# One load, two pieces and GpSimd's scaling for the forget gates of an attention and feed-forward kernel

## The chip, the cores and the metric

The kernel runs on one core of a Trainium2 chip. A core has five engines that run side by side, each with its own queue of instructions: TensorE (PE in the profile, PEld for its weight loads), VectorE (DVE), ScalarE (ACT), GpSimd (POOL) and SyncE (SP), which here only issues transfers (DMAs). They wait for each other by semaphores. The metric is the time of one execution on the device in microseconds (us); lower is better.

## The reference

For 8 batches and 8 heads the reference computes causal attention with a learned decay, and feeds the result through a low-rank token mix and a two-layer perceptron:

```
scores = q @ k^T / 8                                  (576 x 576 per head)
cum    = cumsum(log(clip(f, 1e-4, 1)))                (f: 8 x 8 x 576 forget gates)
attn   = softmax(causal(scores + cum[:, None] - cum[None, :]))
x      = attn @ v                                     (heads side by side: 8 x 576 x 512)
u      = x + (x^T @ U @ V)^T                          (rank 32)
out    = u + relu(u @ w_ch1) @ w_ch2                  (512 -> 2048 -> 512)
```

The softmax runs over the columns of a row, so cum of the row drops out; what is added to the scores is minus cum of the column. Only this matters here: `f` is small (64 rows of 576 numbers), and its clipped, logged and summed form `cum` is needed before the first softmax can be taken.

## The kernel before, in words

Two heads make a pair; there are 32 pairs, and a pair's two heads lie on partitions 0 to 63 and 64 to 127. The attention of the pairs, and the first 6 of 16 column blocks of the perceptron, run in the first some 740 us; the rest of the perceptron follows. The change touches only the beginning.

The beginning (lines 903 to 945) is written by hand, in this order:

- TensorE: 12 products of a constant (line 904), then products of the identity that only keep it running (`keep_awake`, line 868), then the first scores of pair 0. For the pairs 0 and 1 a block of scores is two products for each head: q with k (line 538), and a selector with the sums of the gates (line 544), which adds -8 times `cum` of the pair's head in the same PSUM bank. The selector is the tile `picks`, the sums are the tile `fr`.
- SyncE: loads the gates `f` into `fr` twice, once onto each half of the partitions (line 906); then k, q and the last rows of q of pair 0, the first block of w1, and so on.
- VectorE clips `fr` (line 931), ScalarE takes its logarithm into `fl` (line 932), VectorE sums along the row with a scan back into `fr` (line 934), then writes -8 times the first 64 rows into `fl` (line 935). SyncE stores that to the DRAM tensor `cumd` (line 945), from which the pairs from 2 on load their decay: `decay`, for line 500.
- GpSimd meanwhile fills the masks of pairs 0 and 1 with `affine_select`: four triangles (line 513, in widths of 1024, 512, 256 and 768 columns) and two corners (line 517), then clears rows of `xn` (line 937).

From there on the order of the instructions comes from a planner in the kernel (`run`). Each piece of work is an `op` with a planned duration on one or more engines, a priority and keys that it reads and writes; the planner keeps a clock for each engine and takes the op with the best priority among those that could start. Keys that the hand-written beginning makes, such as `("fr",)` and `("fl",)`, are declared with `known` and a planned time. The engines then run each its own list in that order, and wait where the data is not there yet.

The first softmax work of pair 0 is VectorE's line 556 (add the mask, take the extreme of a row), then ScalarE's line 562 (exponential). Beside it the weights are unpacked: line 385 on ScalarE, 397, 398, 402 and 403 on VectorE, 413 and 417 on GpSimd.

Of the kernel before, what the change touches and what calls it, by code (L numbers as in the profile page):

```python
# [22 lines left out]
P = 128  # L23
# [13 lines left out]
NF = 6  # L37
# [14 lines left out]
def tile_decay_attention_moe(ctx, tc, qk, v, f, U, V, w1, w2, out):  # L52
# [154 lines left out]
    FB_ = [psF.tile([P, 512], F32, tag="F", name=f"F{x}") for x in range(2)]  # L207
    busy = FB_[0]
    still = ident.bitcast(BF16)
    NP = B * NHP  # L210
    cur = [UH, UL]

# [19 lines left out]
    def op(alts, pr, r=(), w=(), opens=(), uses=(), mode=None, lands=None, behind=(), ease=0.0):  # L232
        o = Op()
        o.alts, o.pr, o.opens, o.uses, o.mode, o.lands = alts, pr, opens, uses, mode, lands
        o.gives, o.ready, o.n, o.end, o.group = [], 0.0, state["n"], None, state["group"]
        state["n"] += 1
        need = set()
        for k in r:
            if k in writer:
                need.add(writer[k])  # L240
        for k in w:
            if k in writer:
                need.add(writer[k])
            need.update(readers.get(k, ()))
        for k in r:
            readers.setdefault(k, []).append(o)
        for k in w:
            writer[k], readers[k] = o, []
        need.discard(o)
        o.needs, o.ease = 0, ease  # L250
        for k in behind:
            x = writer.get(k)
            if x is not None and x.end is None and x not in need:
                o.needs += 1
                x.gives.append((o, False))
        for x in need:
            if x.end is None:
                o.needs += 1
                x.gives.append((o, True))
            else:  # L260
                o.ready = max(o.ready, x.end)
        for bank in (*opens, *uses):
            bank.left += 1
        todo.append(o)
        return o
# [10 lines left out]
    def load(pr, nbytes, fn, r=(), w=()):  # L276
        return op([("SP", 0.45, fn)], pr, r, w, lands=nbytes / 200e3)
# [205 lines left out]
    def inputs(p):  # L483
        raw, R = RAW[p % 2], ("raw", p % 2)
        if p:
            pr = p - 1.5
            load(pr, 295e3, lambda: nc.sync.dma_start(raw[:, KO:QW], qk[p, :, 1]), w=[(R, "k")])
            load(pr, 262e3, lambda: nc.sync.dma_start(raw[:, 0:MAIN], qk[p, :, 0, 0:MAIN]), w=[(R, "q")])
            for j in range(2):
                load(pr, 16e3, lambda j=j: nc.sync.dma_start(raw[OWN[j], QT + 64 * j : QT + 64 * j + 64], qk[p, OWN[j], 0, MAIN:S]), w=[(R, "t", j)])  # L490
        if p >= NF:
            h, l = Q
            for n, c, k in ((S, slice(KO, QW), ["k"]), (KO, slice(0, KO), ["q", "t"])):
                kr = [(R, "k")] if k == ["k"] else [(R, "q"), (R, "t", 0), (R, "t", 1)]
                op([("ACT", 0.06 + 0.00088 * n, lambda c=c: nc.scalar.copy(h[:, c], raw[:, c]))], p - 0.5, kr, [("qh", k[0]), ("fr",)])  # L495
                op([("POOL", 0.1 + 0.00225 * n, lambda c=c: nc.gpsimd.tensor_tensor(l[:, c], raw[:, c], h.bitcast(F32)[:, c], op=ALU.subtract))],  # L496
                   p - 0.5, kr + [("qh", k[0])], [("ql", k[0]), *(("picks", x) for x in range(NPK))])
        if p >= NPK:
            src = cumd.rearrange("(j p) s -> p j s", j=2)[p, :, 0:MAIN]
            load(p - 1.0, 524e3, lambda: nc.sync.dma_start(decay, src.unsqueeze(0).broadcast_to([P, 2, MAIN])), r=[("cumd",)], w=[("decay",)])  # L500
            for j in range(2):
                load(p - 0.9, 147e3, lambda j=j: nc.sync.dma_start(Mt[OWN[j]], cumd[j * NP + p].unsqueeze(0).broadcast_to([64, S])), r=[("cumd",)], w=[("Mt", j)])
            for i, d in ((3, 1.0), (1, 0.57), (0, 0.37), (2, 0.79)):
                op([("POOL", d, lambda i=i: triangle(i))], p - 0.4, [("decay",)], [("M", i)])
            for j in range(2):
                op([("POOL", 0.24, lambda j=j: corner(j))], p - 0.3, (), [("Mt", j)])
        vr = VR[p % 2]
        load(p - 0.6, 262e3, lambda: nc.sync.dma_start(vr[:, 0:NM], v[p, 0:MAIN].rearrange("(c p) d -> p c d", p=P)), w=[("vr", p % 2, 0)])
        load(p - 0.6, 33e3, lambda: nc.sync.dma_start(vr[64:128, NM], v[p, MAIN:S]), w=[("vr", p % 2, 1)])
# [15 lines left out]
    def scores(p, parts, pr):  # L525
        ts, bank = terms(p), [Bank("S") for _ in range(2 * len(parts))]
        items = [(i, off, bank[2 * x : 2 * x + 2]) for x, part in enumerate(parts) for i, off in part]
        nm, sm = NMX[p % 2], SMX[p % 2]
        R = ("raw", p % 2)
        kr = [(R, "k"), (R, "q")] if p < NF else [("qh", "k"), ("qh", "q"), ("ql", "k"), ("ql", "q")]  # L530
        cost = sum(P * (i + 1) * (0.00168 if p < NF else 0.00136) + 0.02 for i, _, _ in items) * (2 if p < NPK else 1)

        def go():
            for i, off, own in items:
                w = P * (i + 1)
                for m, (q, k) in enumerate(ts):
                    for j in range(2):
                        nc.tensor.matmul(  # L538
                            own[j][:, off : off + w], q[OWN[j], P * i : P * i + P], k[OWN[j], KO : KO + w],
                            start=m == 0, stop=p >= NPK and m == len(ts) - 1,  # L540
                        )
                if p < NPK:
                    for j in range(2):
                        nc.tensor.matmul(
                            own[j][:, off : off + w], picks[OWN[j], p, 0:P], fr[OWN[j], 0:w], start=False, stop=True
                        )

        op([("PE", cost, go)], pr, kr + ([("fr",), ("picks", p)] if p < NPK else []), [(own[j], i) for i, _, own in items for j in range(2)], opens=bank, mode="S")
        for i, off, own in items:
            w = P * (i + 1)  # L550
            for j in range(2):
                col = 2 * i + j

                def top(own=own, i=i, j=j, off=off, w=w, col=col):
                    ps = own[j][:, off : off + w]
                    nc.vector.tensor_tensor_reduce(  # L556
                        ps, ps, Ms[i][:, j], scale=-SCALE, scalar=3.0e38,
                        op0=ALU.add, op1=ALU.min, accum_out=nm[:, col : col + 1],
                    )

                def use(own=own, i=i, j=j, off=off, w=w, col=col):
                    nc.scalar.activation(  # L562
                        PP[i][j], own[j][:, off : off + w], AF.Exp, bias=nm[:, col : col + 1], scale=-1.0, accum_out=sm[:, col : col + 1]
                    )

                op([("DVE", 0.075 + 0.00105 * w, top)], pr + 0.02, [("M", i)], [(own[j], i), ("nm", p % 2, col)], uses=[own[j]])
                op([("ACT", 0.23 + 0.00088 * w, use)], pr + 0.03, [(own[j], i), ("nm", p % 2, col)], [("P", i, j), ("sm", p % 2, col)], uses=[own[j]])

    def score_tail(p, pr):
# [13 lines left out]
                if p < NPK:  # L583
                    nc.tensor.matmul(ps, picks[:, p, P : 2 * P], fr[:, HW * x : HW * x + HW], start=False, stop=True)

        op([("PE", 0.96 * (2 if p < NPK else 1) if p < NF else 0.8, go)], pr, kr + ([("fr",), ("picks", p)] if p < NPK else []), [(bank[x], 4) for x in range(2)], opens=bank, mode="F")
        for x in range(2):

            def top(x=x):
# [312 lines left out]
    with tc.manual_schedule(engines=None):  # L902
        for _ in range(12):
            nc.tensor.matmul(busy, warm[:, 0:P], warm, start=True, stop=True)
        for j in range(2):
            nc.sync.dma_start(fr[OWN[j]], f)
        raw = RAW[0]
        nc.sync.dma_start(raw[:, KO:QW], qk[0, :, 1])
        nc.sync.dma_start(raw[:, 0:MAIN], qk[0, :, 0, 0:MAIN])
# [18 lines left out]

        for x in range(4):
            pick(0, x)  # L930
        nc.vector.tensor_scalar(fr, fr, 1e-4, 1.0, op0=ALU.max, op1=ALU.min)
        nc.scalar.activation(fl, fr, AF.Ln)
        nc.scalar.activation(fl0, warm[:, P : P + 1], AF.Exp)
        nc.vector.tensor_tensor_scan(fr, fl, fl, 0.0, op0=ALU.add, op1=ALU.bypass)
        nc.vector.tensor_scalar(fl[0 : B * H], fr[0 : B * H], -8.0, None, op0=ALU.mult)
        for i in range(NX - 1):
            nc.gpsimd.memset(xn[i][64:128, NM, :], 0.0)
        known(7.2, ("fr",), ("picks", 0))
        known(7.7, ("fl",), ("warm",))
        known(6.3, (("raw", 0), "k"), (("raw", 0), "q"), (("raw", 0), "t", 0), (("raw", 0), "t", 1))  # L940
        known(5.6, *(("M", i) for i in range(NM)), ("Mt", 0), ("Mt", 1))
        clock.update(PE=6.3, DVE=7.5, ACT=5.4, POOL=6.6, SP=2.7)
        state["pipe"] = 6.0

        load(0.0, 147e3, lambda: nc.sync.dma_start(cumd, fl[0 : B * H]), r=[("fl",)] + [("xl", h) for h in range(2)], w=[("cumd",)])
        for p in range(1, NPK):
            op([("ACT", 1.0, lambda p=p: [pick(p, x) for x in range(4)])], p - 0.6, [("warm",)], [("picks", p)])
# [653 lines left out]
```

## Time and profile before

| what | value |
|---|---|
| median of 3 runs | 1169.71 us (1167.19 to 1170.69) |
| profiled execution: time, and its span | 1169.24 us, 1167.3 us |
| busy over the span: PE, DVE, ACT, POOL | 1144.9, 838.9, 656.8, 312.6 us |
| granted clock of TensorE, mean over the span | 0.998 of full speed |

The span goes from the first to the last instruction that the profile records; the execution's own time has 1.94 us more around it. A busy PE is one that has a product in its pipeline, so that 98% busy does not say that it runs at its peak. In a timeline each row is an instruction, or some equal ones that follow each other: start, duration, engine, line, operation, output and inputs, shapes, and how many. In square brackets stands how long the engine sat idle before the row, and what ended that. PEld is TensorE's loading of weights, which lies beside products that still run; an idle PEld is not an idle PE.

### The profile page before, as it was taken

What the parts mean: (1) busy time and instruction counts of PE and PEld (TensorE: products, weight loads), DVE (VectorE), ACT (ScalarE), POOL (GpSimd) and SP (SyncE); (2) the same over time, 40 slices, a digit from 0 to 9 for tenths busy, and PEclk for the clock granted to TensorE, in tenths of its full rate; (3) what the DMA queues carried; (4) which work ended last, traced back from release to release, by engine and by line L of the source; (5) the groups of instructions that cost most, each with busy time, mean ns of one, the idle gap of its engine ahead of it and who ended that gap; (6) DMA issues with size and microseconds to landing.
All of it is one profiled execution on the core that took longest, in us unless ns stands there. A gap on an engine that the chain in (4) does not pass through costs nothing. (4 is left out here: it accounts for less than half of the span.)

```text
span 1167.3 us, 23653 instructions
## 1 busy us (share of the span) xinstructions
PE 1144.9 (98%) x8380; PEld 999.9 (86%) x8380; DVE 838.9 (72%) x2052; ACT 656.8 (56%) x1760; POOL 312.6 (27%) x439
## 2 busy tenths in 40 slices
PE   9989999999999999999999999999999999999997
PEld 6658778888888888878788898788999999999997
DVE  7999886796786787776877423277777768687765
ACT  7877665666665656665475211246555565655653
POOL 5676554344543436434243000000000000000000
PEclk9999999999999999999999999999999999999999
DMA  6757546555665655566361659347747475564643
GB/s 216 187 156 225 151 145 204 154 182 179 188 196 151 182 189 163 151 208 190 123 201 57 224 191 306 117 160 233 245 158 232 153 248 170 190 214 145 196 117 109
DMA packets 133446, 210.30 MB, mean 180 GB/s; under 512 B 16656, under 2 KB 58896, under 8 KB 131280
## 3 DMA queue, kind: packets, MB, share of 16 engines
q1 hardware_dynamic: 133056, 208.53, 57.2%
q8 instruction: 66, 1.08, 0.4%
q14 instruction: 52, 0.43, 0.1%
q10 hardware_dynamic: 272, 0.26, 0.1%
HBM read 153.03 MB, written 55.72 MB: 179 GB/s over the span
## 5 line engine op out<-in xcount | busy, mean ns | idle before, releaser
L562 ACT ACTIVATE P<-S,nm 128x512 f32<-128x512 f32 (+3 forms) x256 | 132.8, 528 | 62.7 <-DVE nm L556 62.1
L1392 POOL TENSOR_TENSOR xn<-xn,xn 128x512 f32<-128x512 f32 x1 | 1.3, 1267 | 518.7 <-DMA out_dram<-xn 518.7
L556 DVE CUSTOM_DVE_ANT_0 S<-S,M 128x512 f32<-128x512 f32 (+3 forms) x256 | 119.3, 515 | 27.1 <-PE S L538 23.1
L513 POOL TENSOR_SCALAR_AFFINE_SELECT M<-decay 128x1024 f32<-128x1024 f32 (+1 forms) x124 | 93.6, 776 | 108.8 <-DVE nm L556 71.7
L807 PE MATMUL F<-uh,w1h 128*128 128x256 f32 (+1 forms) x344 | 107.4, 312 | 1.1 <-DVE hl L811 1.1
L807 PE MATMUL F<-ul,w1h 128*128 128x256 f32 (+1 forms) x344 | 101.2, 294 | 0.0
L807 PE MATMUL F<-uh,w1l 128*128 128x256 f32 (+1 forms) x344 | 101.1, 294 | 0.0
L274 ACT COPY PT<-T 128x256 f32<-128x256 f32 (+4 forms) x203 | 79.9, 425 | 37.3 <-PE T L629 19.0
L496 POOL TENSOR_TENSOR qkl<-raw,qkh 128x576 fp32r<-128x576 f32 (+1 forms) x52 | 79.5, 1530 | 78.2 <-ACT qkh L495 50.6
L666 PE MATMUL T<-PT,vr 128*64 128x320 f32 (+3 forms) x628 | 90.6, 434 | 2.6 <-DVE PT L274 2.6
L629 PE MATMUL T<-ident,P 128*128 128x128 f32 x614 | 88.0, 275 | 3.3 <-DVE xn L688 2.4
L1464 ACT COPY ost<-pf 128x512 f32<-128x512 f32 x70 | 41.1, 587 | 87.4 <-PE pf L1241 87.4
L1464 ACT COPY mc<-pf 128x512 f32<-128x512 f32 x69 | 40.5, 587 | 81.5 <-PE pf L1241 79.6
L629 PEld LDWEIGHTS T<-ident,P 128*128 128x128 f32 x614 | 69.9, 140 | 18.2 <-DVE xn L688 3.4
L828 PE MATMUL F<-w2h,hh 128*128 128x512 f32 x198 | 84.7, 428 | 0.4 <-DVE ul L754 0.4
L666 PEld LDWEIGHTS T<-PT,vr 128*64 128x64 f32 x628 | 40.7, 138 | 47.6 <-issue 34.1
L828 PE MATMUL F<-w2l,hh 128*128 128x512 f32 x198 | 77.9, 393 | 0.0
L828 PE MATMUL F<-w2h,hl 128*128 128x512 f32 x198 | 77.3, 390 | 0.0
L274 DVE COPY PT<-T 128x512 f32<-128x512 f32 (+4 forms) x103 | 51.4, 506 | 33.9 <-PE T L629 12.0
L1241 PE MATMUL pf<-d,b1h 128*128 128x256 f32 x320 | 69.5, 280 | 0.0
L807 PEld LDWEIGHTS F<-uh,w1h 128*128 128x128 f32 x344 | 65.3, 190 | 4.0 <-DVE hl L811 1.5
L816 ACT ACTIVATE hh<-F 128x256 fp32r<-128x256 f32 (+1 forms) x86 | 34.6, 411 | 56.4 <-PE F L807 56.1
(354 smaller groups left out, 3588.4 us busy)
## 6 DMA issues: line engine op xcount, KB each, us to landing
un<-ud SPq DMA_DIRECT2D x16, 1024.0 KB, 6.5
decay<-cumd SPq DMA_DIRECT2D x30, 512.0 KB, 6.3
d<-ud SPq DMA_DIRECT2D x48, 256.0 KB, 3.8
araw<-in_w_dram SPq DMA_DIRECT2D x20, 512.0 KB, 4.8
wd<-araw SPq DMA_DIRECT2D x20, 512.0 KB, 3.0
raw<-in_qk_dram SPq DMA_DIRECT2D x32, 288.0 KB, 4.2
Th<-twd SPq DMA_DIRECT2D x35, 256.0 KB, 3.6
tw<-twd SPq DMA_DIRECT2D x35, 256.0 KB, 3.0
```

The costliest lines, as they stand in the source:

```text
L274: return [("ACT", 0.133 + 0.00068 * n, lambda: nc.scalar.copy(dst(), src())), ("DVE", 0.064 + 0.00104 * n, lambda: nc.vector.tensor_copy(d ...
L496: op([("POOL", 0.1 + 0.00225 * n, lambda c=c: nc.gpsimd.tensor_tensor(l[:, c], raw[:, c], h.bitcast(F32)[:, c], op=ALU.subtract))], p - 0. ...
L513: nc.gpsimd.affine_select(Ms[i], decay[:, :, 0:w], [[0, 2], [-1, w]], ALU.is_ge, MASKED, base=P * i, channel_multiplier=1)
L556: nc.vector.tensor_tensor_reduce(ps, ps, Ms[i][:, j], scale=-SCALE, scalar=3.0e38, op0=ALU.add, op1=ALU.min, accum_out=nm[:, col : col + 1],)
L562: nc.scalar.activation(PP[i][j], own[j][:, off : off + w], AF.Exp, bias=nm[:, col : col + 1], scale=-1.0, accum_out=sm[:, col : col + 1])
L629: nc.tensor.transpose(bank[:, P * x : P * x + P], PP[i][j][:, P * c : P * c + P], ident)
L666: nc.tensor.matmul(ps, vr[:, c, j], PT[:, j, c, lo:hi], start=c == 0, stop=lo == 0)
L807: nc.tensor.matmul(bank[:, :nt], wt[:, fc, c], ut[:, c, sl], start=m == 0, stop=m == 3 * NDC - 1)
L816: op([("ACT", 0.133 + 0.00066 * nt, lambda: nc.scalar.activation(HH[:, fc, :nt], bank[:, :nt], AF.Relu))], pr, [(bank, 0)], [("hh", fc)], ...
L828: nc.tensor.matmul(bank[:, :], ht[:, fc, P * y : P * y + P], wt[:, fc], start=fc == 0 and m == 0, stop=fc == NA - 1 and m == 2,)
L1241: nc.tensor.matmul(ps, a[x][:, c], b[y][:, c], start=start and m == 0, stop=m == 5, skip_group_check=True)
L1464: nc.scalar.copy(mc, FA)
```

## The change

The gates are loaded by one DMA that reads `f` twice. Clip and logarithm, and after them the sum, go in two pieces of columns, 0 to 255 and 256 to 575; the second sum starts from the last column of the first. The key `("fr",)` becomes one key for each piece; a block of scores asks for the pieces that its columns need. The scaling by -8 leaves VectorE's hand-written beginning, and becomes an op of the planner on GpSimd, planned at 0.8 us, on which the store of `cumd` waits.

```
@@ -207,6 +207,7 @@
+    PIECES = ((0, 2 * P), (2 * P, S))
@@ -545,7 +546,8 @@  (scores)
-        op([("PE", cost, go)], pr, kr + ([("fr",), ("picks", p)] if p < NPK else []), [(own[j], i) for i, _, own in items for j in range(2)], opens=bank, mode="S")
+        upto = [("fr", x) for x, (c0, c1) in enumerate(PIECES) if any(P * (i + 1) > c0 for i, _, _ in items)]
+        op([("PE", cost, go)], pr, kr + ([*upto, ("picks", p)] if p < NPK else []), [(own[j], i) for i, _, own in items for j in range(2)], opens=bank, mode="S")
...
@@ -902,8 +904,7 @@
-        for j in range(2):
-            nc.sync.dma_start(fr[OWN[j]], f)
+        nc.sync.dma_start(fr, f.unsqueeze(0).broadcast_to([2, B * H, S]))
...
@@ -928,20 +929,24 @@
-        nc.vector.tensor_scalar(fr, fr, 1e-4, 1.0, op0=ALU.max, op1=ALU.min)
-        nc.scalar.activation(fl, fr, AF.Ln)
+        for x, (c0, c1) in enumerate(PIECES):
+            c = slice(c0, c1)
+            nc.vector.tensor_scalar(fr[:, c], fr[:, c], 1e-4, 1.0, op0=ALU.max, op1=ALU.min)
+            nc.scalar.activation(fl[:, c], fr[:, c], AF.Ln)
         nc.scalar.activation(fl0, warm[:, P : P + 1], AF.Exp)
-        nc.vector.tensor_tensor_scan(fr, fl, fl, 0.0, op0=ALU.add, op1=ALU.bypass)
-        nc.vector.tensor_scalar(fl[0 : B * H], fr[0 : B * H], -8.0, None, op0=ALU.mult)
+        for x, (c0, c1) in enumerate(PIECES):
+            c = slice(c0, c1)
+            nc.vector.tensor_tensor_scan(fr[:, c], fl[:, c], fl[:, c], fr[:, c0 - 1 : c0] if c0 else 0.0, op0=ALU.add, op1=ALU.bypass)
...
-        known(7.2, ("fr",), ("picks", 0))
+        known(7.2, ("fr", 0), ("fr", 1), ("picks", 0))
...
+        op([("POOL", 0.8, lambda: nc.gpsimd.tensor_scalar(fl[0 : B * H], fr[0 : B * H], -8.0, None, op0=ALU.mult))], 0.2, [("fr", 0), ("fr", 1)], [("fl",)] + [("xl", h) for h in range(2)])
         load(0.0, 147e3, lambda: nc.sync.dma_start(cumd, fl[0 : B * H]), r=[("fl",)] + [("xl", h) for h in range(2)], w=[("cumd",)])
```

VectorE's list at the beginning, from the last constant to the first softmax work of pair 0, stands so in the kernel before (S is a bank of scores, nm the extremes of its rows, M a mask):

```order
L125 MEMSET warm 128x128
L931 TENSOR_SCALAR fr<-fr 128x576
L934 SCALAR_TENSOR_TENSOR fr<-fl 128x576
L935 TENSOR_SCALAR fl<-fr 64x576
L556 ISA S_142,nm_129<-S_142,M_113 128x512
L556 ISA nm_129 128x1
```

and so in the changed one, where lines of the file have moved by one to five (558 is 556 of before):

```order
L125 MEMSET warm 128x128
L934 TENSOR_SCALAR fr<-fr 128x256
L934 TENSOR_SCALAR fr<-fr 128x320
L939 SCALAR_TENSOR_TENSOR fr<-fl 128x256
L939 SCALAR_TENSOR_TENSOR fr<-fl,fr 128x320
L558 ISA S_142,nm_129<-S_142,M_113 128x512
L558 ISA nm_129 128x1
```

Clip and scan are two instructions each, and the scaling is gone from here. GpSimd's list from its last triangle to the first weights, before (`stg` holds raw weights, w1l is the low part of an unpacked block of w1):

```order
L513 AFFINE_SELECT M_112<-decay 128x768
L517 AFFINE_SELECT Mt<-Mt 64x64 x2
L937 MEMSET xn_97 64x512
L937 MEMSET xn_98 64x512
L413 TENSOR_TENSOR stg_202<-stg_202 128x512
L417 TENSOR_TENSOR w1l<-stg_202,w1h 128x512
```

and after the change (414 is 413 of before):

```order
L514 AFFINE_SELECT M_112<-decay 128x768
L518 AFFINE_SELECT Mt<-Mt 64x64 x2
L941 MEMSET xn_97 64x512
L941 MEMSET xn_98 64x512
L949 TENSOR_SCALAR fl<-fr 64x576
L414 TENSOR_TENSOR stg_203<-stg_203 128x512
L418 TENSOR_TENSOR w1l<-stg_203,w1h 128x512
```

The scaling stands behind the two clears, ahead of the first weights. ScalarE has two logarithms in place of one, and SyncE one load in place of two. Every other instruction of all five lists, to the end of the kernel, stands in the same order in both programs.

## Rows read from the trace of the kernel before

**Rows 1.** The page's first part: busy time, share of the span, instructions.

```profile
PE 1144.9 (98%) x8380; PEld 999.9 (86%) x8380; DVE 838.9 (72%) x2052; ACT 656.8 (56%) x1760; POOL 312.6 (27%) x439
```

**Rows 2.** Busy time by stretch: window, length, then PE, PEld, DVE, ACT, POOL.

```profile
16.75:30.00 13.25, 13.25 (x93) 8.70 (x92) 12.87 (x41) 9.67 (x32) 6.97 (x11) 1.00 0.66 220
```

**Rows 3.** Timeline of TensorE, first scores of pair 0.

```profile
5.88 0.82 PE L868 MATMUL F<-ident 128*128 128x256 bf16 x6
6.62 1.13 PE L538 MATMUL S<-raw 64*128 64x512 f32 x4
...
7.49 0.37 PEld L544 LDWEIGHTS S<-fr,picks 64*128 64x128 f32 x4 [0.57 <-DVE fr L934]
7.59 1.10 PE L544 MATMUL S<-fr,picks 64*128 64x512 f32 x4
```

**Rows 4.** Timeline of TensorE, the same work of pair 1.

```profile
16.75 1.13 PE L538 MATMUL S<-raw 64*128 64x512 f32 x4
17.71 1.02 PE L544 MATMUL S<-fr,picks 64*128 64x512 f32 x4
```

**Rows 5.** Timeline of VectorE from the gates' clip to the first weights.

```profile
4.64 0.54 DVE L931 TENSOR_SCALAR fr<-fr 128x576 f32<-128x576 f32 x1 [2.82 <-DMA fr<-in_f_dram]
5.93 1.50 DVE L934 TENSOR_TENSOR_SCAN fr<-fl 128x576 f32<-128x576 f32 x1 [0.75 <-ACT fl L932]
7.47 0.45 DVE L935 TENSOR_SCALAR fl<-fr 64x576 f32<-64x576 f32 x1
8.77 0.70 DVE L556 CUSTOM_DVE_ANT_0 S<-S,M 128x512 f32<-128x512 f32 x1 [0.84 <-PE S L544]
...
10.03 0.43 DVE L397 TENSOR_SCALAR stg<-stg 128x512 int32<-128x512 int32 x1
```

**Rows 6.** Timeline of ScalarE up to the logarithm.

```profile
3.29 1.42 ACT L927 ACTIVATE picks<-warm,ident 64x128 f32<-64x128 bf16 x4 [1.06 <-POOL ident masks.py:199]
5.21 0.69 ACT L932 ACTIVATE fl<-fr 128x576 f32<-128x576 f32 x1 [0.50 <-DVE fr L931]
```

**Rows 7.** Timeline of GpSimd: triangles, a corner, a clear; last a later corner.

```profile
4.22 0.61 POOL L513 TENSOR_SCALAR_AFFINE_SELECT M<-decay 128x512 f32<-128x512 f32 x1
4.79 0.65 POOL L513 TENSOR_SCALAR_AFFINE_SELECT M<-decay 128x256 f32<-128x256 f32 x1
5.40 0.83 POOL L513 TENSOR_SCALAR_AFFINE_SELECT M<-decay 128x768 f32<-128x768 f32 x1
6.19 1.28 POOL L517 TENSOR_SCALAR_AFFINE_SELECT Mt<-Mt 64x64 f32<-64x64 f32 x1
...
8.44 0.52 POOL L937 MEMSET xn<- 64x512 f32 x1
...
33.02 0.23 POOL L517 TENSOR_SCALAR_AFFINE_SELECT Mt<-Mt 64x64 f32<-64x64 f32 x1
```

**Rows 8.** Timeline of SyncE's issues.

```profile
0.74 1.22 SPq L906 DMA_DIRECT2D fr<-in_f_dram  x2
...
8.95 0.47 SPq L945 DMA_DIRECT2D cumd<-fl  x1
...
12.68 0.52 SPq L490 DMA_DIRECT2D raw<-in_qk_dram  x1
14.96 0.35 SPq L487 DMA_DIRECT2D raw<-in_qk_dram  x1
...
17.04 0.38 SPq L500 DMA_DIRECT2D decay<-cumd  x1
```

**Rows 9.** Issue to landing: of the tile fr, then of the store of cumd.

```profile
DMA to landing us min/median/max: 2.8/3.0/3.1
...
cumd<-fl SPq DMA_DIRECT2D x1, 144.0 KB, 5.1
```

**Rows 10.** GpSimd's groups by shape: times, then busy us and mean ns.

```profile
L496 POOL TENSOR_TENSOR qkl<-raw,qkh 128x576 fp32r<-128x576 f32 x26 | 37.7, 1449 | 73.0 <-ACT qkh L495 46.8 <-PE T L629 22.3 <-PE F L761 3.7
L914 POOL MEMSET Mt<- 128x576 f32 x1 | 0.6, 571 | 0.0
```

More of the change, by code (lines that the diff above doesn't have):

```diff
@@ L494, in inputs @@
                 kr = [(R, "k")] if k == ["k"] else [(R, "q"), (R, "t", 0), (R, "t", 1)]
-                op([("ACT", 0.06 + 0.00088 * n, lambda c=c: nc.scalar.copy(h[:, c], raw[:, c]))], p - 0.5, kr, [("qh", k[0]), ("fr",)])
+                op([("ACT", 0.06 + 0.00088 * n, lambda c=c: nc.scalar.copy(h[:, c], raw[:, c]))], p - 0.5, kr, [("qh", k[0]), ("fr", 0), ("fr", 1)])
                 op([("POOL", 0.1 + 0.00225 * n, lambda c=c: nc.gpsimd.tensor_tensor(l[:, c], raw[:, c], h.bitcast(F32)[:, c], op=ALU.subtract))],
@@ L584, in go @@
                     nc.tensor.matmul(ps, picks[:, p, P : 2 * P], fr[:, HW * x : HW * x + HW], start=False, stop=True)
-        op([("PE", 0.96 * (2 if p < NPK else 1) if p < NF else 0.8, go)], pr, kr + ([("fr",), ("picks", p)] if p < NPK else []), [(bank[x], 4) for x in range(2)], opens=bank, mode="F")
+        op([("PE", 0.96 * (2 if p < NPK else 1) if p < NF else 0.8, go)], pr, kr + ([("fr", 0), ("fr", 1), ("picks", p)] if p < NPK else []), [(bank[x], 4) for x in range(2)], opens=bank, mode="F")
         for x in range(2):
```

## The prediction

> **What bounds the kernel now.** I read the busy times first: TensorE is busy 98% of the span [rows 1]. A change that touches only the beginning can move the end only if it moves TensorE's or VectorE's work there, so the beginning is to be read instruction by instruction. The stretches come next: from 16.75 to 30 us TensorE is busy for all of 13.25 us and VectorE for 12.87 [rows 2]. Neither has slack to catch up in, so what is won or lost before 16.75 us is mostly carried on. I therefore price every shift of the first softmax work, VectorE's line 556 at 8.77 us, at its full size.
>
> What sets that 8.77? VectorE sat idle 0.84 us before it, waiting for TensorE's line 544 [rows 5]. TensorE itself runs the identity products from 5.88 us, starts the scores at 6.62, and the products with the gates' sums at 7.59 [rows 3]. Here the view can mislead. It says that the weight loads of line 544 sat idle for 0.57 us and that VectorE's scan of `fr` ended this. But from the start of line 538 to that of line 544 it is 7.59 - 6.62 = 0.97 us. In pair 1, where `fr` is more than 9 us old and cannot be waited for, the same step takes 17.71 - 16.75 = 0.96 us [rows 4]. So the four products of line 538 fill the time; only the loading of weights was late, beside products still in the pipeline. TensorE waited for the gates 0.01 us.
>
> It was close, though: the scan ends at 5.93 + 1.50 = 7.43 us, and the weight loads start at 7.49 [rows 3, 5]. The chain of the gates has no gain to give, and hardly any room to get later.
>
> **The change part by part.**
>
> *One load for two.* Two issues cost SyncE 1.22 us [rows 8], so one goes, 0.6 us. The gates land 2.8 to 3.1 us after an issue [rows 9]: from an issue at 0.74 that is 3.5 to 3.8 us, against a clip that began at 4.64 [rows 5]. The one load carries as many bytes as the two; if its landing were stretched by the bytes of the second, it would land where the second landed before. So: 0 to 0.7 us earlier. The loads behind it, k and q of pair 0 among them, come 0.6 us earlier too. This is worth nothing, because TensorE is filled by the identity products until it starts line 538 [rows 3], and its list is the same.
>
> *Clip and logarithm in pieces.* The first logarithm cannot start before the picks are made, at 3.29 + 1.42 = 4.71 us [rows 6]; before, it started at 5.21. By columns, 256 and 320 of 576, the 0.69 us become 0.31 and 0.38, plus a start for the second piece. There is no row for that start alone; I bound it by 0 and by 0.36 us, a whole pick of 64 to 128 columns (1.42 for four) [rows 6], and take 0.1. So the first piece is there at about 5.1 and the second at about 5.5 us.
>
> *The sum in pieces.* By columns the scan's 1.50 us become 0.67 and 0.84. The first runs from about 5.1 to 5.8, the second to 6.65, with a start of 0.1 to 0.2 to 6.8 us. That is 0.6 us ahead of the 7.43 of before. The second scan waits on VectorE's own first one, and nothing but the first softmax work is queued behind it. Worth at line 544: the 0.01 us above, so nothing. What is late next is TensorE's own line 538.
>
> *The scaling leaves VectorE.* Its 0.45 us at 7.47 lay in the idle time before 8.77 [rows 5]: nothing gained.
>
> *The scaling on GpSimd.* It stands behind the second clear, which ended at 8.44 + 0.52 = 8.96 us [rows 7]. No row of before has this operation at this size. From below, the clear of 128x576 took 0.57 us; from above, an operation with two inputs over 576 columns took 1.45 [rows 10]. I take 0.8, nearer to the lower row, since it has one input. It ends at 9.5 to 10.4, by my value at 9.8 us. GpSimd's next work, line 413, was issued much later, behind VectorE's unpacking. If the scaling still runs when VectorE wants to start line 397 at 10.03 [rows 5], the two may meet; that is taken up among the rivals, and by my value they don't.
>
> *The store of `cumd`* is issued when the scaling is done, at some 9.8 us for 8.95, with bounds of 9.5 and 10.5. Behind it in SyncE's queue stand the loads of U, of v of pair 1 and of pair 2's first raw rows. They are issued back to back until 12.68 + 0.52 = 13.20, and then SyncE waits for TensorE until 14.96 [rows 8]. That is 1.76 us of room for a delay of 0.5 to 1.5, so SyncE is back in step by 14.96. The store lands 5.1 us after its issue [rows 9], at 14.9 (15.6 at worst), and the first read of `cumd` was issued at 17.04 [rows 8]. Hidden, with 1.4 us or more left.
>
> *The sum.* Against the profiled execution, 1167.3 us of span and 1.94 around it: 1169.24 + 0 for the load, clip, logarithm and scan - 0.01 at line 544 + 0 for the scaling and its store = 1169.2 us. The median of the runs stands at 1169.71, 0.47 above the profiled one; the same sum from there is 1169.7. I put the forecast between the two, at 1169.5.
>
> **The rivals.**
>
> *GpSimd comes between the pieces: slower by 0.2 to 0.8 us.* The trace shows that VectorE's operations on the gates and GpSimd's selects shut each other out. The corner at 6.19 us took 1.28 us and so ended at 7.47, when the scan did (7.43); the same shape later took 0.23 [rows 7]. The triangle at 4.79, of 256 columns, took longer than the one of 512 before it, while the clip ran until 5.18. And the scan, which began at 5.93, had a triangle in front of it until 6.23 [rows 7]: without that wait it ran 1.2 us. [...] Say that the turns alternate. The triangle of 256 columns lies behind the second clip at some 5.4, and takes 0.26 (its 0.65 less the 0.39 of the clip's rest). Then scan one takes 0.53 (256 columns of 1.2 us), from 5.6 to 6.2, the last triangle 0.83 to 7.0, and scan two 0.67 to 7.66. That is 0.23 us behind the old 7.43, and TensorE has no room: line 544 comes 0.2 us late, or 0.5 if the scans take their shares of 1.50. The corners and clears then end at 9.1, and a scaling of 1.45 us at 10.55, with line 397 in its way for up to 0.3. Together +0.2 to +0.8: 1169.4 to 1170.5. The point from which it decides is a second scan that ends after 7.43 us.
>
> [...]
>
> [...]
>
> *The lead of the gates reaches TensorE: faster by up to 0.6 us.* This would be so if line 544 had waited after all, by the 0.57 us that the view gives its weight loads, less the 0.1 us that loading takes in any case: 1169.24 - 0.5 = 1168.7. Against it stands pair 1 with its 0.96.
>
> *The store of `cumd` comes too late: slower by 1 us or more.* It would need a scaling that ends after 8.95 + 1.76 = 10.7 us, for instance because it is twice as slow as a two-input operation. At 2.9 us from 9.1 it ends at 12.0, SyncE is 1.3 us late at 14.96, and if all of it reached the scores of pair 2 the time would be 1170.5. For it speaks only that this operation was never seen at this size.
>
> *The change does not do what it says*: the one load could be no faster than the two. Then the gates are clipped from 4.64 us, the first logarithm starts at about 4.95, and the second scan still ends by 7.1: no change.
>
> **How the numbers follow.** No effect on the end (within 0.2 us), 65%; GpSimd between the pieces, 20%; the lead reaches TensorE, 6%; the late store, 5%; something that no view here shows, 4%, as much in either direction. A measurement can tell about 0.3% of this kernel's time from no change, 3.5 us, and all cases but the last lie well within that. So faster and slower get 3% each, the half of the unseen one and a little for the scatter of the runs, which reached 3.5 us from the lowest to the highest. The range is set by that scatter more than by the change: from 1167.2, the lowest run of before, to 1172.0, the highest plus the 1.3 us of the late store.
>
> **What would show it.** In the changed profile: one issue of `fr` and a clip that starts near 4.0 us; the second scan ending before 7.43; line 544 of before starting at 7.59 and the first softmax work at 8.77, both within 0.05; the scaling on GpSimd between 8 and 10.5 us with a duration of 0.57 to 1.45; the store of `cumd` issued right behind it; SyncE's issue of 14.96 where it was. I am wrong if line 544 starts before 7.5 or after 7.7, if line 397 waits for GpSimd, or if the issue at 14.96 has moved by more than the first softmax work. A time beyond 3.5 us on either side, with all of these in place, would mean that the cause lies in a stretch which this change does not touch.

## The result, and the profile after

The changed kernel is slower, and by more than the scatter of the runs:

| | median | lowest to highest | runs |
|---|---|---|---|
| before | 1170.07 us | 1167.19 to 1170.69 | 6 |
| changed | 1176.61 us | 1175.49 to 1176.93 | 6 |

The ratio is 1.0057, with a 95% interval of 1.0047 to 1.0067: about 6.6 us more. The profiled execution took 1175.5 us, with a span of 1173.6 (1169.24 and 1167.3 before). I had forecast 1169.5 us in a range of 1167.2 to 1172.0, and gave "slower" 3%.

VectorE's timeline of the changed kernel shows at once where to look. It answers to [rows 5]; line 934 is the clip in two pieces, 939 the scans, 558 the first softmax work (556 of before).

```profile
10.48 0.53 DVE L934 TENSOR_SCALAR fr<-fr 128x256 f32<-128x256 f32 x2 [8.66 <-DMA fr<-in_f_dram]
11.25 0.69 DVE L939 TENSOR_TENSOR_SCAN fr<-fl 128x256 f32<-128x256 f32 x1 [0.25 <-ACT fl L935]
12.05 0.88 DVE L939 TENSOR_TENSOR_SCAN fr<-fl,fr 128x320 f32<-128x320 f32 x1
15.91 0.70 DVE L558 CUSTOM_DVE_ANT_0 S<-S,M 128x512 f32<-128x512 f32 x1 [2.98 <-PE S L545]
```

The clip waits 8.66 us for the gates and starts at 10.48 us, where it started at 4.64. The first softmax work starts at 15.91 instead of 8.77, 7.14 us late. That is more than the whole loss, and it is there after 16 us.

The timeline of TensorE, for [rows 3] (870 is 868 of before, 539 is 538, 545 is 544):

```profile
6.97 1.03 PE L870 MATMUL F<-ident 128*128 128x256 bf16 x6
12.01 2.08 PE L539 MATMUL S<-raw 64*128 64x512 f32 x4 [4.01 <-DMA raw<-in_qk_dram]
13.85 1.95 PE L545 MATMUL S<-fr,picks 64*128 64x512 f32 x4
```

TensorE does not wait for the gates here either: the second scan ends at 12.05 + 0.88 = 12.93 us, and line 545 starts at 13.85, right behind line 539. What it waits for is k and q of pair 0, for 4.01 us. Their issues, by size, with the time from issue to landing:

```profile
raw<-in_qk_dram SPq DMA_DIRECT2D x1, 288.0 KB, 9.7
raw<-in_qk_dram SPq DMA_DIRECT2D x1, 256.0 KB, 9.9
```

and before:

```profile
raw<-in_qk_dram SPq DMA_DIRECT2D x1, 288.0 KB, 3.1
raw<-in_qk_dram SPq DMA_DIRECT2D x1, 256.0 KB, 3.2
```

So k and q, which the change does not touch, landed 9.7 and 9.9 us after their issue, for 3.1 and 3.2 before. SyncE's issues, for [rows 8]:

```profile
0.73 0.73 SPq L907 DMA_DIRECT2D fr<-in_f_dram  x1
...
4.79 1.76 SPq L510 DMA_DIRECT2D vr<-in_v_dram  x1
10.47 0.33 SPq L488 DMA_DIRECT2D raw<-in_qk_dram  x1
...
14.72 0.47 SPq L950 DMA_DIRECT2D cumd<-fl  x1
```

Between 6.55 and 10.47 SyncE issues nothing: its next load waits for the completion of the gates' load, the eighth before it, as the view of waits has it (who waited for what, us in total, times, longest):

```profile
SPq L488 <- DMA fr<-in_f_dram: 3.9, 1, 3.9
```

The stretches of one microsecond say what the transfers did meanwhile. The columns are the window, its length, busy time of PE, PEld, DVE, ACT and POOL, then TensorE's granted clock, the busy share of the 16 DMA engines, and GB/s.

```profile
7.00:8.00 1.00, 1.00 (x7) 0.57 (x5) 0.00 (x0) 0.00 (x0) 0.40 (x1) 1.00 0.97 257
8.00:9.00 1.00, 0.00 (x0) 0.00 (x0) 0.00 (x0) 0.00 (x0) 0.00 (x0) 1.00 0.25 64
9.00:10.00 1.00, 0.00 (x0) 0.00 (x0) 0.00 (x0) 0.00 (x0) 0.00 (x0) 1.00 0.13 48
10.00:11.00 1.00, 0.00 (x0) 0.00 (x0) 0.52 (x2) 0.20 (x1) 0.00 (x0) 0.90 0.13 50
11.00:12.00 1.00, 0.00 (x0) 0.02 (x1) 0.70 (x2) 0.98 (x3) 0.00 (x0) 0.50 0.56 119
12.00:13.00 1.00, 0.99 (x2) 0.52 (x4) 0.88 (x1) 0.99 (x2) 0.00 (x0) 0.50 0.91 326
```

The reader is to see two things. From 9 to 11 us the transfers are busy to 0.13 of 16 engines, which is 2.1 engines, and move 48 to 50 GB/s, some 24 for each. By this share two of sixteen DMA engines work and fourteen stand still (an estimate: the trace does not name the engine of a packet), while every compute engine waits until the clip at 10.48. And TensorE, idle from 8.0 us, is granted 0.50 of its clock from 11 us on; line 539 takes 13.85 - 12.01 = 1.84 us where it took 0.97.

The lag, by where a line starts first in the two traces: 7.1 us at the first softmax work; 8.0 at line 688, the first finished rows of pair 0 (34.7 for 26.7); 7.1 at line 807, the first layer of the perceptron (97.3 for 90.2); 6.6 at line 1241 (753.8 for 747.2); 6.3 at the end of the span. Of 8.0 us, 1.7 come back in the course of the kernel.

Of these 1.7 us, 1.1 go with a chance of the two executions. VectorE's instruction that started at 80.50 us before is 7.62 us late in the changed kernel (88.12), the one of 100.10 only 6.52 (106.62). Just ahead of this TensorE's granted clock read 0.50 from 76.5 to 79.5 us in the profiled execution of before, and 1.00 in that of the changed kernel; first two stretches of before, then one of the changed kernel, with the columns as above:

```profile
76.00:78.00 2.00, 0.96 (x4) 0.45 (x6) 1.94 (x4) 0.00 (x0) 1.94 (x5) 0.61 0.00 0
78.00:80.00 2.00, 2.00 (x10) 0.59 (x8) 1.94 (x6) 1.83 (x5) 1.75 (x3) 0.54 0.00 0
...
76.00:88.00 12.00, 9.37 (x77) 7.00 (x76) 11.75 (x17) 6.53 (x18) 10.86 (x13) 1.00 0.29 92
```

That fits the clock as the cause of the 1.1 us; no run here changed it alone.

### The profile page after: what moved, and what is told of

Read it like the earlier page. It is cut to its first block, busy times and chain, and to the rows that moved or that the text cites. A ratio compares the mean times of both kernels' runs of the same rounds, so it can differ in the third digit from the quotient of the medians.

```text
span 1173.6 us, 23654 instructions
## 1 busy us (share of the span) xinstructions
PE 1147.5 (98%) x8380; PEld 1000.9 (85%) x8380; DVE 838.4 (71%) x2053; ACT 656.3 (56%) x1761; POOL 312.1 (27%) x440
## 5 line engine op out<-in xcount | busy, mean ns | idle before, releaser
L497 POOL TENSOR_TENSOR qkl<-raw,qkh 128x576 fp32r<-128x576 f32 (+1 forms) x52 | 79.6, 1532 | 79.5 <-ACT qkh L496 51.1
L275 DVE COPY PT<-T 128x512 f32<-128x512 f32 (+4 forms) x103 | 51.5, 506 | 34.7 <-PE T L631 12.9
```

What stands on the lines that cost most here:

```text
L275: return [("ACT", 0.133 + 0.00068 * n, lambda: nc.scalar.copy(dst(), src())), ("DVE", 0.064 + 0.00104 * n, lambda: nc.vector.tensor_copy(d ...
```

## The experiments

Theory S: the one load reads `f.unsqueeze(0).broadcast_to([2, 64, 576])`, and with its outermost extent of 2 it runs over 2 DMA engines. Its 295 KB at the 48 GB/s measured from 9 to 10 us take 6.1 us (an estimate), and the parts of k and q that lie on the same two engines queue behind them. The landings agree: k came at 1.52 + 9.7 = 11.2 us, 0.7 behind the gates' clip, and q at 1.98 + 9.9 = 11.9, another 0.7. An estimate from the rows above, for loads that are spread evenly over sixteen engines: a sixteenth of 288 KB at 24 GB/s is 0.77 us, of 256 KB 0.68. Its rivals: L, GpSimd gets between the pieces; Q, the scaling on GpSimd, which took 1.67 us, and the late store; R, reading the same rows twice is what is slow. Each run was timed against the kernel before on the same chip.

**The two loads put back** into the changed kernel.

```
-        nc.sync.dma_start(fr, f.unsqueeze(0).broadcast_to([2, B * H, S]))
+        for j in range(2):
+            nc.sync.dma_start(fr[OWN[j]], f)
```

> The changed kernel with the two loads of the gates put back; pieces and GpSimd's scaling stay. Theory S (the one load, with its 2 as the outermost extent of its source, moves over 2 of the 16 DMA engines; the gates and the k and q queued behind them come late): clip at about 4.6 us, first softmax work at 8.7 to 9.2, 1169.5 to 1170.9 us. Rival L (GpSimd between the two pieces) and rival Q (the scaling on GpSimd took 1.67 us and its store comes late): the loss stays, 1174 us or more.

Measured: 1169.45 us, ratio 0.9993 (0.9983 to 1.0003). Its VectorE:

```profile
4.26 1.98 DVE L935 TENSOR_SCALAR fr<-fr 128x256 f32<-128x256 f32 x2 [2.44 <-DMA fr<-in_f_dram]
...
6.98 0.89 DVE L940 TENSOR_TENSOR_SCAN fr<-fl,fr 128x320 f32<-128x320 f32 x1
9.88 0.70 DVE L558 CUSTOM_DVE_ANT_0 S<-S,M 128x512 f32<-128x512 f32 x1 [2.01 <-PE S L545]
```

The loss is gone with the one load; pieces and scaling together cost nothing that can be told. The first softmax work came at 9.88, later than I expected; the section on the prediction comes back to it.

**The one load alone** in the kernel before: the same edit the other way.

> The kernel before with the one load alone; clip, logarithm and sum in one piece, scaling on VectorE. S: clip at 10 to 11 us, first softmax work at 15.5 to 17, 1175.5 to 1178 us, the whole loss or a little more. L and Q: 1169 to 1171 us.

Measured: 1176.72 us, ratio 1.0062 (1.0045 to 1.0079).

```profile
10.29 0.46 DVE L930 TENSOR_SCALAR fr<-fr 128x576 f32<-128x576 f32 x1 [8.46 <-DMA fr<-in_f_dram]
...
15.73 0.70 DVE L556 CUSTOM_DVE_ANT_0 S<-S,M 128x512 f32<-128x512 f32 x1 [2.39 <-PE S L544]
```

The whole loss, without pieces or GpSimd. L and Q fall.

**The scaling on GpSimd alone** in the kernel before.

```
-        nc.vector.tensor_scalar(fl[0 : B * H], fr[0 : B * H], -8.0, None, op0=ALU.mult)
+        op([("POOL", 0.8, lambda: nc.gpsimd.tensor_scalar(fl[0 : B * H], fr[0 : B * H], -8.0, None, op0=ALU.mult))], 0.2, [("fr",)], [("fl",)] + [("xl", h) for h in range(2)])
```

> The kernel before with the scaling on GpSimd alone; two loads, no pieces. S: 1169 to 1171 us, the scaling starts at about 9.0 and ends at about 10.6, line 397 on VectorE late by at most 0.6, the store of cumd issued near 10.7 and SyncE in step again at about 15.0. Q: the store holds up SyncE, 1172 us or more.

Measured: 1169.15 us, ratio 0.9999 (0.9989 to 1.0008). GpSimd's scaling:

```profile
8.80 1.67 POOL L944 TENSOR_SCALAR fl<-fr 64x576 f32<-64x576 f32 x1
```

and SyncE's store of `cumd`, the wait for TensorE that was at 14.96 [rows 8], and the first read of `cumd`:

```profile
10.50 0.47 SPq L945 DMA_DIRECT2D cumd<-fl  x1
...
15.50 0.35 SPq L487 DMA_DIRECT2D raw<-in_qk_dram  x1
...
17.52 0.43 SPq L500 DMA_DIRECT2D decay<-cumd  x1
```

The store is 1.55 us later, and SyncE is back in step: it issues 0.54 us later than before, and TensorE's first scores came 0.56 later in this run (7.18 for 6.62). The room did hide it.

**One load of 128 rows.** The gates lie twice in DRAM, laid out before the launch, so that the load has no step of 0 and 128 as its outermost extent.

```
-        nc.sync.dma_start(fr, f.unsqueeze(0).broadcast_to([2, B * H, S]))
+        nc.sync.dma_start(fr, f)
-        "f": f.reshape(NP, 2, S).transpose(1, 0, 2).reshape(2 * NP, S),
+        "f": np.tile(f.reshape(NP, 2, S).transpose(1, 0, 2).reshape(2 * NP, S), (2, 1)),
```

> The changed kernel, but the gates lie twice in DRAM (128 rows, laid out before the launch), so that the one load has 128 rows as its outermost extent and reads nothing twice. S: gates on time, clip at about 4.0 us, second scan done before 7.5, first softmax work at 8.7 to 9.9, 1168.8 to 1170.9 us. Rival R (reading the same rows twice is what is slow): the same. L or Q: 1174 us or more.

Measured: 1170.16 us, ratio 1.0002 (0.9992 to 1.0011).

```profile
3.80 2.46 DVE L934 TENSOR_SCALAR fr<-fr 128x256 f32<-128x256 f32 x2 [1.98 <-DMA fr<-in_f_dram]
6.17 0.71 DVE L939 TENSOR_TENSOR_SCAN fr<-fl 128x256 f32<-128x256 f32 x1
7.00 0.88 DVE L939 TENSOR_TENSOR_SCAN fr<-fl,fr 128x320 f32<-128x320 f32 x1
```

The gates land early, as I had forecast of the change itself (clip at 3.80 for 4.64), and nothing is gained. The second scan ends at 7.88, later than the 7.5 that I expected. This run speaks for S, but R would expect the same. The next three tell them apart.

**The outermost extent as a dose: 2, 4 and 16 blocks.** The gates lie twice in DRAM, in blocks with an unused row of zeros behind each, so that no row is read twice and yet the load's source keeps three steps, such as `[2, 64, 576]`. For two blocks:

```
+        nc.sync.dma_start(fr, f[:, 0:64])
+        "f": np.pad(np.tile(f.reshape(NP, 2, S).transpose(1, 0, 2).reshape(2 * NP, S), (2, 1)).reshape(2, 64, S), ((0, 0), (0, 1), (0, 0))),
```

> The changed kernel, but the gates lie twice in DRAM as two blocks of 64 rows with an unused row behind each, so that the one load has the outermost extent 2 as in the changed kernel and yet reads nothing twice. S (split by the outermost extent, 2 of 16 DMA engines): clip at 10 to 11 us, 1175.5 to 1178 us, as the changed kernel. R (reading the same rows twice is slow): clip at about 4.0, 1168.8 to 1170.9 us.

> As the last, in four blocks of 32 rows: outermost extent 4. S: 4 DMA engines carry 74 KB each instead of 147, at the 23 GB/s that one showed in the changed kernel 3.2 us instead of 6.4, so the clip starts at about 7.3 us instead of 10.5, and the time is 1171 to 1174 us, between the kernels. R: clip at about 4.0, 1168.8 to 1170.9 us. A theory by which any such three-step source is slow, whatever its extent: as with two blocks.

> As the last, in sixteen blocks of 8 rows: outermost extent 16. S: all 16 DMA engines, clip at about 4.0 to 4.3 us, 1168.8 to 1170.9 us. A theory by which any such three-step source is slow: clip after 7 us, 1172 us or more.

| outermost extent | clip starts | time | ratio (interval) |
|---|---|---|---|
| 2 | 10.22 us | 1176.46 us | 1.0060 (1.0043 to 1.0076) |
| 4 | 7.81 us | 1172.73 us | 1.0027 (1.0018 to 1.0036) |
| 16 | 4.38 us | 1170.02 us | 1.0000 (0.9991 to 1.0009) |

The clip's row in the three, for two, four and sixteen blocks:

```profile
10.22 0.53 DVE L934 TENSOR_SCALAR fr<-fr 128x256 f32<-128x256 f32 x2 [8.40 <-DMA fr<-in_f_dram]
```

```profile
7.81 0.53 DVE L934 TENSOR_SCALAR fr<-fr 128x256 f32<-128x256 f32 x2 [5.99 <-DMA fr<-in_f_dram]
```

```profile
4.38 1.87 DVE L934 TENSOR_SCALAR fr<-fr 128x256 f32<-128x256 f32 x2 [2.56 <-DMA fr<-in_f_dram]
```

Two blocks without any row read twice are as slow as the change, so R falls; from 9 to 11 us their transfers are busy to 0.13 of 16 engines and move 48 to 50 GB/s, the figures of the changed kernel. Four blocks lie between, with the clip 0.5 us behind what S expected. Sixteen are as good as the kernel before, so that the three steps by themselves are not slow. S stands, as a reading of these starts: that four blocks run on four engines and sixteen on sixteen, no stretch of the traces shows on its own.

**The load behind k and q.** The changed kernel, with the one load issued after the raw loads of pair 0.

> The changed kernel with its one load issued behind k, q and the last rows of q of pair 0. S: k and q land at 5 to 6 us, so that line 538 of before starts at 6.6 to 7.8, while the gates, issued at about 3.2, land at 11.5 to 13 and hold line 544 until 14 to 15.5; TensorE waits between them and the time is 1176 to 1179 us, no better than the changed kernel. A theory by which only k and q matter, queued behind the gates: 1170 to 1172 us.

Measured: 1177.48 us, ratio 1.0064 (1.0049 to 1.0079).

```profile
7.15 1.13 PE L539 MATMUL S<-raw 64*128 64x512 f32 x4
15.07 2.08 PE L545 MATMUL S<-fr,picks 64*128 64x512 f32 x4 [6.79 <-DVE fr L939]
```

Now k and q are in time, and TensorE waits 6.79 us for the gates instead. So late gates alone are enough for the loss; in the changed kernel, where TensorE waits for k and q and not for the gates, it is what queues behind them.

**TensorE kept at work while it waits.** The changed kernel with 36 more products of the identity (18 calls of `keep_awake`) ahead of the first scores.

```
-                    for _ in range(int((est - clock["PE"] - 0.15) / 0.24)):
+                    more = 0 if "awake" in state else 18
+                    state["awake"] = True
+                    for _ in range(more + int((est - clock["PE"] - 0.15) / 0.24)):
```

> The changed kernel with 36 more products of the identity on TensorE in front of the first scores, so that it works while it waits for k and q. If the half clock behind the idle 4 us costs on its own: the scores start at about 12.0 us as in the changed kernel, but at full clock, the first softmax work comes at about 14.2 instead of 15.9, and the time is 1174 to 1175.8 us, some 1 to 1.7 less than the changed kernel. If the clock costs nothing in the end (VectorE and later waits take it up): 1176 to 1177 us.

Measured: 1173.65 us, ratio 1.0036 (1.0023 to 1.0049), against 1.0057 for the changed kernel.

```profile
6.72 4.75 PE L872 MATMUL F<-ident 128*128 128x256 bf16 x42
12.05 1.13 PE L541 MATMUL S<-raw 64*128 64x512 f32 x4 [0.58 <-DMA raw<-in_qk_dram]
13.03 1.13 PE L547 MATMUL S<-fr,picks 64*128 64x512 f32 x4
```

k and q land as late as in the changed kernel, but line 541 now takes 0.98 us to its successor instead of 1.84, and the first softmax work starts at 14.31 instead of 15.91. By the ratios, 0.0021 of the time comes back, some 2.5 us of the 6.6; their intervals together allow 0.5 to 4.4 (an estimate), so that the 1 to 1.7 that I expected are not excluded.

The two profiled executions show 2.4 us. From 14 to 16 us TensorE has 0.50 of its clock in the changed kernel (first row) and all of it here (second row; after the window and its length, PE, the granted clock, the DMA share and GB/s):

```profile
14.00:16.00 2.00, 2.00 (x9) 0.50 0.86 258
14.00:16.00 2.00, 2.00 (x24) 1.00 0.80 271
```

By line 688 of before (690 in the changed kernel, 692 here) the lead has grown from 1.6 us to 34.68 - 32.26 = 2.42:

```profile
26.71 0.68 DVE L688 TENSOR_TENSOR xn<-T,rv 128x512 f32<-128x512 f32 x1
34.68 0.68 DVE L690 TENSOR_TENSOR xn<-T,rv 128x512 f32<-128x512 f32 x1
32.26 0.69 DVE L692 TENSOR_TENSOR xn<-T,rv 128x512 f32<-128x512 f32 x1
```

At the end of the span 1173.6 - 1172.3 = 1.3 us of it are left. Most of the rest goes between 80 and 120 us: at line 737 of the changed kernel (739 here) the lead is 80.7 - 78.2 = 2.5 us at the last row from the bank F and 119.9 - 118.3 = 1.6 at the first from T. What takes it there is not shown.

**A shorter start.** The kernel before with the one load of 128 rows, and 9 instead of 12 constant products (`range(12)` to `range(9)`), as a version that might beat both.

> The kernel before (no pieces, scaling on VectorE) with one load of 128 rows that lie twice in DRAM, and 9 instead of 12 constant products ahead of the first scores. S, and TensorE's list as what sets the first scores: gates clipped at about 3.8, scores start 0.6 to 1.3 us earlier than in the kernels with 12 products, line 544 held by the scan until 7.0 to 7.6, time 1168.6 to 1169.8 us, a gain too small to tell. [...]

Measured: 1169.38 us, ratio 0.9998 (0.9990 to 1.0007): no difference. Three products fewer, and the scores still started at 7.10 us:

```profile
1.87 4.02 PE L904 MATMUL F<-warm 128*128 128x512 bf16 x9 [1.87 <-DVE warm L125]
5.69 1.49 PE L868 MATMUL F<-ident 128*128 128x256 bf16 x6
7.10 1.27 PE L538 MATMUL S<-raw 64*128 64x512 f32 x4
```

The nine took 4.02 us, where the twelve took 4.16 in the profiled execution of before, and the six identity products 1.49 for 0.82: each product took longer. The time lies in the expected range of 1168.6 to 1169.8; the scores did not start 0.6 to 1.3 us earlier. I found no version that beats the kernel before by a measurable amount.

## Why the prediction was wrong, point by point

*One load for two: the step that failed.* I wrote that the one load "carries as many bytes as the two; if its landing were stretched by the bytes of the second, it would land where the second landed before. So: 0 to 0.7 us earlier." This took for granted that bytes alone set the landing, and that the one load is spread as the two were. It was not: with the copy dimension of 2 in front, the transfers from 9 to 11 us were busy to 0.13 of 16 engines, 2.1 of them, at 48 to 50 GB/s. The clip came 5.8 us later instead of 0 to 0.7 earlier. My bound on the bad side, no later than before, had no row under it, since no row of before showed a load with so small an outermost extent; it should have been open. The rival in which the change does not do what it says had the same flaw: it let the load be no faster, and never slower.

*The loads behind it* were said to come 0.6 us earlier. They were issued 0.5 and 0.65 us earlier, and landed after 9.7 and 9.9 us, at 11.2 and 11.9, behind the gates that were clipped from 10.48. The term was wrong for the same reason.

*What bounds the beginning.* That TensorE did not wait for the gates is right of the profiled execution. That it stands filled by its own list until 6.62 us holds only while k and q are there, and only for that execution: the first twelve products took 4.16 us in it, and between 4.71 and 5.28 in the other executions with gates in time. There the first scores started at 7.18, 7.51, 7.54 and 7.74 us for 6.62, and the times of these kernels don't differ measurably. The room for the gates was larger than it looked.

*Pieces.* The sizes were right where GpSimd was idle: in the changed kernel clip to second scan took 12.93 - 10.48 = 2.45 us, against 7.43 - 4.64 = 2.79 in one piece. With GpSimd at its selects, as in the run with one load of 128 rows, it took 7.88 - 3.80 = 4.08 us, and the two clips 2.46 instead of 0.53. That the turns alternate between the scans, as the first rival's sum supposes, no run shows: the time went at the clips, and the scans took 0.71 and 0.88 there, for 0.69 and 0.88 in the changed kernel. Nor does a run show the 1.2 us that I gave the scan without its wait: with the one load alone, where GpSimd had long been done, it took 1.36. The second scan ended after 7.43, that rival's point of decision. It cost nothing measurable, since the scores started at 7.51 and line 545 at 8.47 in that run. The rival's 1169.4 to 1170.5 us add 0.2 to the profiled time and 0.8 to the median; from the profiled time alone the upper end is 1170.0.

*The scaling on GpSimd* was mis-sized: 1.67 us, in every run that has it, above my upper bound of 1.45. That it and the late store are hidden was right: the run with it alone is at 0.9999. VectorE's line 397 never waited for it. In two traces, one load of 128 rows and sixteen blocks, the view puts VectorE's wait before the first softmax work down to the scaling, which ended at about that moment. But from the start of line 545 to that work it is 9.64 - 8.47 = 1.17 us with 128 rows, and 8.77 - 7.59 = 1.18 before, so that TensorE accounts for it.

*Carried on at full size.* Of 7.14 us at the first softmax work, 6.3 stood at the end of the span, and most of the difference goes with the stretch in which before had 0.61 and 0.54 of the clock and the changed kernel 1.00. That part held for the large lag, and it is why 6 us at the beginning are seen at all. For small ones it is not shown: with the two loads put back the first softmax work came 1.11 us late and the span ended 0.2 us late (1167.5 for 1167.3); with sixteen blocks it came 0.91 late and ended 1.0 late (1168.3).

*The half clock*, 0.50 behind the idle wait of 4.01 us, was in none of my cases. The run with TensorE kept at work prices it at about 2.4 us in the trace and 2.5 by the ratios, with 0.5 to 4.4 allowed: some third of the loss, known roughly.

## What to carry to other kernels

When two transfers are made one, look at the outermost extent of its access pattern, not only at its bytes: here the clip of the gates started at 10.48 us behind a copy dimension of 2 in front, at 7.81 behind four blocks and at 4.38 behind sixteen, and k and q, issued behind the copy dimension of 2, landed after 9.7 and 9.9 us for 3.1 and 3.2. A term that has no row under it needs a bound on the bad side as well, and in a kernel whose busiest engine hardly catches up, as here, a late first load can cost nearly all of its lateness: of 7.14 us at the first softmax work 6.3 were left at the end, and by the ratios some 2.5 us of the loss go with the clock of 0.50 on TensorE behind its wait of 4.01 us. Before a few tenths of a microsecond of room are read from one profiled execution, look at a second one: the first scores started at 6.62 us here and at 7.74 in a kernel with the same list for TensorE and no measurable difference in the time.

## What the runs showed of the hardware that I had not expected

- From 9 to 11 us of the changed kernel the transfers were busy to 0.13 of 16 engines, 2.1 of them, and moved 48 to 50 GB/s: some 24 GB/s for each busy engine, an estimate from these two figures. k and q, issued behind the gates, landed 9.7 and 9.9 us after their issue, for 3.1 and 3.2 in the kernel before and 3.3 and 3.6 in the run with one load of 128 rows.
- The moment from which TensorE's first products come faster differs between executions of the same list: twelve equal products took 4.16 us in the profiled execution of before, 5.04 with one load of 128 rows, and 5.28 with the two loads put back, without a difference in the time of the three kernels. The shortest, the median and the longest of the twelve in ns, before and in the changed kernel, where they took 5.30 us:

```profile
L904 PE MATMUL F<-warm x12: 379/576/631, 1.9 to 5.7; 128*128 128x512 bf16 x12
L906 PE MATMUL F<-warm x12: 609/634/634, 1.9 to 6.5; 128*128 128x512 bf16 x12
```

  The granted clock reads 1.00 from 2 to 7 us before, in the changed kernel and with one load of 128 rows; what makes the products faster is not shown.
- TensorE's granted clock fell to 0.50 while it stood idle for 4.01 us (the changed kernel) and for 4.17 (two blocks); in a wait of 2.05 us (four blocks) it stayed at 1.00. Behind waits of 4.61 us (the one load alone) and 6.79 (the load behind k and q) the first four products took 13.66 - 11.82 = 1.84 and 16.93 - 15.07 = 1.86 us to their successors; with the gates in time these steps took 0.97 (before) and 9.33 - 8.47 = 0.86 (one load of 128 rows).
- GpSimd needed 1.67 us for an operation with one input over 64x576, more than the 1.45 us that one with two inputs over 128x576 took [rows 10].
